# Weight unpacking, half of the score masks and the gate's carried columns leave VectorE, in a newly drawn order

## The chip, the cores and the metric

The kernel runs on one NeuronCore of a Trainium2 chip. Five engines work from queues of their own: TensorE (PE in the profile; PEld is its weight loads), VectorE (DVE), ScalarE (ACT), GpSimd (POOL) and SyncE (SP), which issues all the DMAs. An engine takes its instructions strictly in the order in which the program holds them. The metric is the device time of one execution in microseconds (us).

## The reference

Two layers, all in float32. The first is a recurrence over 768 time steps, for 4 batches and 8 heads of size 40; the second is a gated layer with a width-3 convolution.

```python
for t in range(S):                                   # attention part, B=4 H=8 S=768 D=40
    y[:, :, t] = einsum('bhd,bhde->bhe', rt, state)
    Sa = einsum('bhde,bhe->bhd', state, at)
    state = state * wt[:, :, None, :] - einsum('bhd,bhe->bhde', Sa, bt)
    state = state + einsum('bhd,bhe->bhde', vt, kt)

x = y.transpose(0, 2, 1, 3).reshape(B, S, H * D)     # [4, 768, 320]
h = maximum(x @ w_in, 0)                             # d_ff = 1024
conv = sum_k conv_w[k] * h_padded[:, k:k+S]          # 3 taps along time
out = (h / (1 + exp(-conv))) @ w_out
```

The weights `w_in`, `conv_w` and `w_out` come as float64 words, and the kernel turns them into float32 itself.

## The kernel before

The recurrence is cut into 24 chunks of 32 steps (`C = 32`). Inside a chunk it is written as matrices: scores between the chunk's vectors, a triangular system of 32 unknowns, and a state that is handed from chunk to chunk. Two neighbouring chunks form a pair (12 of them) and share loads, decays and one solve. The gated layer works on 12 windows of 64 steps, each in four quarters (`fp`) of the 1024 columns.

The work is cut into short parts, each a Python generator that stops at every `yield`:

- `we` (weights): a weight piece of 120 or 128 rows by 256 columns. The load, then `from_f64` (L211 to L236) on VectorE with eight instructions, the last two a product `ef` (L232) and a sum `tf` (L235); then ScalarE rounds it to the high part (L253) and GpSimd subtracts for the low part (L255). There are 23 pieces with the convolution's; two can be on their way at a time.
- `de`, `dd` (decays, decayed): running products of `w` by VectorE's scans (L369, L376) and the scaled `a`, `k`, `b`.
- `sc` (scores): products of `a` with `k` and `b` (tile `ps`), masked by VectorE into `at` (L437). `at[:, c, 0]` is for `k`, `at[:, c, 1]` for `b`.
- `si`, `so` (solve_in, solve): the `b` half of the scores goes through DRAM (`bd`) and comes back as `bb`, one system on each partition; the solve is then 31 steps of two elementwise instructions (L480, L486), followed by stores and loads through DRAM (`xd`, `tt`). `VSOL` says which solves run on VectorE; the others run on GpSimd.
- `ch` (chain): the step of the recurrence. TensorE's products `pp`, `pu` and `pn`, VectorE's sum of the state (L562), GpSimd's product with the decay (L568).
- `rt`, `vt`, `ut`, `st`, `pa`, `ou`, `fi` (rturn, vturn, uturn, sturn, pairs, outputs, finish): the chunk's output, scaled and split into a high and a low part (`xh`, `xl`; L665, L667) for the gated layer.
- `pk`, `mi`, `mo` (pack, moe_in, moe_out): per window a few copies by DMA, then per quarter eight float32r products for each of two column blocks (`ph`, L700), Relu on ScalarE into `hb` (L714), the three taps (L721 on ScalarE, L729 on VectorE), the sigmoid (L734), the gate's product (L736), its split (L740, L743), and the output matmuls (`po`, L754). `hb` holds two columns more than the window, carried from the window before: L712 copies them in from `hend`, L716 copies the new last two out.

What sets the order is a list of tokens written by hand or drawn by a planner, `ORDER`: `de1.0` advances part 0 of the decays of pair 1 to its next `yield`, `so0*2` advances solve 0 by two pieces. `emit_all` goes through the list and emits the instructions in just that order, and `put` only enforces what must precede what. So each engine's queue is the list as far as it concerns that engine.

```python
VSOL = range(0, 12, 2)
...
    def advance(key):
        a = acts[key]
        for other, n in a[3].get(a[2], ()):
            while acts[other][2] < n:
                advance(other)
```

Of the kernel before, what the change touches and what calls it, by code (L numbers as in the profile page):

```python
# [20 lines left out]
VSOL = range(0, 12, 2)  # L21
# [18 lines left out]
    st1*2 sc4 we6 so1 we8*4 we9 we10 ch1 lv3 rt1 we9 st1*2 ut1 pa1 lr2 ou1 ha4 ld3*2 we10 so1*3 fi0  # L40
    vt2 we10 fi0 fi1 de3.0 sc4 sc5 we9 we10 sc5 ch1 de3.1 we9 de3.1 ha4 we11 we12 lr3 rt2 fi1 st2*2
    fi1 we11 we12 we11*2 ro0 we13 we12*2 ha5 st2 we13 we14 ha5 ld4 so1 we13 dd3.0*3 dd3.1*3 we14*2
    ch2 si2 so2 ch2 pk0 ut2 so2*2 pa2 vt3 sc6 so2*2 st2 ou2 ch2 ro0 rt3 mi0.0*3 so2*2 mi0.0*2 ch2
    st3*2 we13 mi0.1*2 st3 ld4 so2 ld4 we14 lv4 we15 we16 ch3*2 sc6 sc7 ut3 we15 st3 we15 sc7 fi2*3
    lr4 mi0.0 pa3 mi0.0 ch3 we15 ch3 we16 mi0.0 we17 mi0.1 mi0.2 we17*2 mi0.2 so2 ch4 si3 we16 so3
    ou3 ha6 we16 we18 de4.0 we18 ha6 ha7 st4 fi3*2 we17 we19 de4.0 we18 mi0.1 we19 vt4 st4*3 lv5
    de4.1 ch4 ut4 so3 ch4 dd4.0 rt4 we18 we20 de4.1 we20 mi0.2 so3 we20 pa4 vt5 ch4 ch5 so3 mi0.2
    ch5 fi3 ha7 we19*2 we21*2 ut5 we20 we22*2 ou4 st5*2 mi0.1 st5 lr5 rt5 so3 we22 ld4 ld5 de5.0
    mi0.1 we21 ch5 we22 mi0.3 we21 mi0.0*2 so3 mi0.1*2 mi0.3 pa5 mi0.3 pk1 dd4.0*2 dd4.1 mi0.1*2
    dd4.1 st5 mi0.2 sc8 fi4*2 ld5 dd4.1 ou5 mi0.2 lv6 mi0.3 so3*2 sc8 mi0.2 sc9 mi0.2*2 ha8*2 ha9  # L50
    fi4 fi5 ld5 de5.0 de5.1 ha9 sc9 mi0.2 dd5.0 mi0.3 dd5.0 de5.1 lv7 mi1.0*3 mi1.1 ld5 dd5.0 dd5.1
    sc10 so3 si4 mi0.3 lr6 dd5.1*2 ch5 mi0.3 lr7 mi0.3 mi1.1*2 mi1.0*3 mi1.1 mi1.2 vt6 sc10 mi0.3
    mo0.0 sc11 mi0.3 mi1.1 mi1.0*2 mi1.1 ch6 st6 mi1.2 ch6*2 sc11 mi1.1*2 mo0.0*2 ch6 mo0.0 mo0.1*5
    ld6 ut6 rt6 ch7 mi1.1 so4 ld6 so4*2 pa6 vt7 st6 fi5*2 st6 so4*2 mi1.0 so4 mi1.2 st6 mi1.3 so4
    mi1.2 so4 lv8 ou6 mi1.0 mo1.0 mi1.2 mi1.3*2 st7*2 ch7 ut7 mi1.1 st7*2 rt7 ch7*2 mo1.0 pa7
    mi1.3*2 fi6*2 pk2 lr8 mi1.2*2 ou7 mi1.2 rt8 so4 si5 ch8 st8*2 mi1.2 mi1.3 mi1.2 mi1.3 ch8*2 lv9
# [946 lines left out]
```

## Time and profile before

| | |
|---|---|
| median of 3 runs | 708.97 us (708.5 to 709.71) |
| the profiled execution | 708.08 us, span 706.4 us |
| busy over the span: TensorE | 560.7 us, 79% |
| VectorE | 538.4 us, 76% |
| ScalarE | 350.7 us, 50% |
| GpSimd | 353.2 us, 50% |
| granted clock of TensorE | 0.906 of full speed |

The span is the time from the first to the last instruction. Rows that name a line give instruction, output and inputs, shapes, count, busy time, the mean in ns, then the idle time of the engine just before them and what ended it. Rows of a window give for each engine the busy time and the number of instructions in it. The profile's slices are 706.4 / 40 = 17.7 us long.

### The profile page before, as it was taken

How to read it: one execution, taken by the hardware profiler on the slowest of the kernel's cores; microseconds unless marked ns; L12 is line 12 of the kernel's file. 1: busy time of each engine (PE TensorE's matmuls, PEld its weight loads, DVE VectorE, ACT ScalarE, POOL GpSimd, SP SyncE). 2: the span in 40 equal slices, each digit the busy share in tenths (PEclk: the TensorE clock that was granted, in tenths of full speed). 3: DMA queues.
4: the chain of work that ended last, by engine and by line, in shares of the span. 5: the costliest groups of instructions: out<-in, count | busy, mean ns of one | idle time of the engine just before them, and what ended most of it. 6: DMA issues, size and time to landing. Idle time of an engine off the chain costs nothing. (4 is left out here: it accounts for less than half of the span.)

```text
span 706.4 us, 29930 instructions
## 1 busy us (share of the span) xinstructions
PE 560.7 (79%) x13021; PEld 497.9 (70%) x13021; DVE 538.4 (76%) x1261; ACT 350.7 (50%) x792; POOL 353.2 (50%) x582
## 2 busy tenths in 40 slices
PE   4444764677687898988977996899998977899886
...
DVE  6689889998999896657795578987979894456571
...
POOL 2001884037786235783234884236985028863321
PEclk9766777997799998989999998999998999999998
...
GB/s 139 120 117 108 103 112 102 95 94 144 22 41 107 56 72 79 94 81 82 82 20 89 86 86 106 81 60 69 89 62 91 6 54 94 29 51 32 21 30 19
DMA packets 242402, 53.40 MB, mean 76 GB/s; under 512 B 229000, under 2 KB 238112, under 8 KB 242272
## 3 DMA queue, kind: packets, MB, share of 16 engines
...
q8 instruction: 102, 1.67, 1.0%
...
## 5 line engine op out<-in xcount | busy, mean ns | idle before, releaser
L729 DVE SCALAR_TENSOR_TENSOR cc<-hb,cw,cc 128x256 f32<-128x256 f32 x192 | 106.3, 575 | 13.7 <-ACT cc L721 10.2
L568 POOL TENSOR_TENSOR s<-s,wc 120x360 f32<-120x360 f32 x88 | 75.8, 891 | 69.4 <-DVE s L562 69.4
L486 POOL TENSOR_TENSOR xx<-xx,st 128x126 f32<-128x126 f32 (+22 forms) x186 | 83.1, 447 | 14.6
L480 POOL TENSOR_TENSOR st<-xx,bb 128x126 f32<-128x126 f32 (+22 forms) x186 | 79.4, 427 | 21.1 <-DMA bb<-bd 8.4
L700 PE MATMUL ph<-xh,wih 120*128 120x256 f32 x288 | 56.6, 306 | 11.3 <-ACT hb L714 11.3
L486 DVE TENSOR_TENSOR xx<-xx,st 128x126 f32<-128x126 f32 (+22 forms) x186 | 54.2, 291 | 6.4
L480 DVE TENSOR_TENSOR st<-xx,bb 128x126 f32<-128x126 f32 (+22 forms) x186 | 53.6, 288 | 7.2 <-DMA bb<-bd 1.7
L736 DVE TENSOR_TENSOR cc<-cc,hb 128x512 f32<-128x512 f32 x48 | 40.8, 857 | 21.7 <-ACT cc L734 21.5
L562 DVE TENSOR_TENSOR s<-pn,s 120x360 f32<-120x360 f32 x88 | 40.6, 522 | 20.6 <-PE pn L549 20.6
L700 PEld LDWEIGHTS ph<-xh,wih 120*128 120x128 f32 x288 | 41.8, 194 | 15.0 <-ACT hb L714 13.1
L734 ACT ACTIVATE cc<-cc 128x512 f32<-128x512 f32 x48 | 30.4, 636 | 43.6 <-DVE cc L729 43.5
L667 POOL TENSOR_TENSOR xl<-xf,xh 120x384 fp32r<-120x384 f32 x24 | 26.8, 1117 | 45.2 <-ACT xh L665 41.5
L721 ACT ACTIVATE cc<-hb,cw 128x256 f32<-128x256 f32 x96 | 43.5, 506 | 8.7 <-DVE hb L712 2.9
L602 PE MATMUL pt<-ident,s 120*120 120x120 f32 x276 | 40.6, 279 | 6.4 <-DVE s L562 3.2
L427 ACT ACTIVATE ap<-ah,hmask 120x384 f32<-120x384 f32 (+1 forms) x72 | 36.6, 576 | 17.4 <-DVE ah L391 10.1
L604 ACT COPY sn<-pt 120x360 f32<-120x360 f32 x92 | 38.9, 471 | 12.2 <-PE pt L602 11.8
L714 ACT ACTIVATE hb<-ph 128x512 f32<-128x512 f32 x48 | 28.8, 600 | 27.2 <-PE ph L700 23.4
L579 ACT ACTIVATE rp<-pr,hmask 120x384 f32<-120x384 f32 x72 | 36.7, 586 | 6.9 <-PE pr L576 6.5
L700 PE MATMUL ph<-xl,wih 120*128 120x256 f32 x192 | 39.3, 287 | 0.0
L533 PE MATMUL pu<-psb,tt 32*32 32x40 f32 x1536 | 22.5, 209 | 19.6 <-ACT psb L527 16.1
L602 PEld LDWEIGHTS pt<-ident,s 120*120 120x120 f32 x276 | 31.2, 143 | 9.0 <-DVE s L562 3.5
L533 PEld LDWEIGHTS pu<-psb,tt 32*32 32x32 f32 x1536 | 18.7, 114 | 24.5 <-ACT psb L527 17.7
...
## 6 DMA issues: line engine op xcount, KB each, us to landing
...
```

The costliest lines, as they stand in the source:

```text
L480: eng.tensor_tensor(t3, xx[:, 0:nj, i : i + 1].to_broadcast([128, nj, nt]), bb[:, i : i + 1, i + 1 :].to_broadcast([128, nj, nt]), ALU.mult,)
L486: eng.tensor_tensor(xx[:, 0:nj, i + 1 :], xx[:, 0:nj, i + 1 :], t3, ALU.add)
L533: nc.tensor.matmul(pu[quad(bi), hc], tt[quad(bi), c, h, :], psb[quad(bi), hc], start=(h == 0), stop=True, skip_group_check=True,)
L562: nc.vector.tensor_tensor(new, pn[bi][:GR], old[bi], ALU.add)
L568: nc.gpsimd.tensor_tensor(n4, n4, w4, ALU.mult)
L579: nc.scalar.activation(out=rp[:, :, h, :], in_=pr[:GR], func=AF.Copy, scale=hmask[:, h : h + 1])
L602: nc.tensor.transpose(pt[:GR, g, :], old[bi][:, g, :], ident[:GR, :GR])
L604: nc.scalar.copy(sn, pt[:GR])
L700: nc.tensor.matmul(ph[:, j], l[:, fs], x, start=(j == 0 and i == 0), stop=(i == len(passes) - 1), skip_group_check=True,)
L721: nc.scalar.activation(out=cc[:, j], in_=hb[:, j, :, 1 : W + 1], func=AF.Copy, scale=cw[:, 1, f : f + 1],)
L729: nc.vector.scalar_tensor_tensor(out=cc[:, j], in0=hb[:, j, :, x : W + x], scalar=cw[:, x, f : f + 1], in1=cc[:, j], op0=ALU.mult, op1=ALU ...
L736: nc.vector.tensor_tensor(cc, cc, hb[:, :, :, 1 : W + 1], ALU.mult)
```

## The change

Three jobs change their engine, and the order is drawn anew.

- In each weight piece ScalarE multiplies the low word `m` by 2^-44, and GpSimd makes the product with `e` and the sum. VectorE keeps six of eight instructions.
- In the scores VectorE masks only the `k` half. ScalarE writes the `b` half with the sign turned and unmasked; the solve reads only the entries that the mask leaves. The signed mask `trin` is gone.
- The gate's copies of the two carried columns, into `hb` and out to `hend`, run on ScalarE.
- `VSOL` goes from the even solves to 0, 3, 5, 7, 9, 11, so solves 1 and 2 both run on GpSimd, and from 3 on the odd ones on VectorE.

```diff
-VSOL = range(0, 12, 2)
+VSOL = (0, 3, 5, 7, 9, 11)
...
 ORDER = """
-    ld0 de0.0*2 ld0*2 de0.1 ld0 ld1 de0.1 we0 dd0.0*3 dd0.1*2 sc0 dd0.1 we0 ld1*2 lr0 sc0 sc1 lr1
+    we0*2 ld0*2 de0.0*2 de0.1*2 ld0 dd0.0*2 ld0 we1 dd0.0 dd0.1*3 we0 sc0 ha0*2 ld1 de1.0 we1 de1.0
...
-    trin = cp.tile([128, 2, 1, C], F32, name="trin")
-    nc.vector.tensor_copy(trin[:, 0, 0], tri)
-    nc.vector.tensor_scalar(
-        out=trin[:, 1, 0], in0=tri, scalar1=-1.0, scalar2=None, op0=ALU.mult
-    )
...
         tf, ef = t.bitcast(F32), e.bitcast(F32)
+        nc.scalar.activation(out=m.bitcast(F32), in_=m, func=AF.Copy, scale=2.0**-44)
         V.scalar_tensor_tensor(out=tf, in0=e, scalar=896.5, in1=tf, op0=ALU.is_ge, op1=ALU.mult)
         V.tensor_scalar(out=e, in0=t, scalar1=-(1 << 23), scalar2=None, op0=ALU.bitwise_and)
-        V.scalar_tensor_tensor(
-            out=ef, in0=m, scalar=2.0**-44, in1=ef, op0=ALU.mult, op1=ALU.mult
-        )
-        V.tensor_tensor(tf, tf, ef, ALU.add)
+        nc.gpsimd.tensor_tensor(ef, m.bitcast(F32), ef, ALU.mult)
+        nc.gpsimd.tensor_tensor(tf, tf, ef, ALU.add)
...
+        nc.scalar.activation(out=at[:, c, 1], in_=ps[:, 1], func=AF.Copy, scale=-1.0)
         nc.vector.tensor_tensor(
-            at[:, c], ps, trin.to_broadcast([128, 2, H, C]), ALU.mult,
+            at[:, c, 0], ps[:, 0], tri.unsqueeze(1).to_broadcast([128, H, C]), ALU.mult,
         )
...
-                    nc.vector.tensor_copy(hb[:, :, :, 0:2], he)
+                    nc.scalar.copy(hb[:, :, :, 0:2], he)
...
-        nc.vector.tensor_copy(he, hb[:, :, :, W : W + 2])
+        nc.scalar.copy(he, hb[:, :, :, W : W + 2])
```

What this does to the queues, at three places. The rows give line, operation, output and inputs, and the output's shape; line numbers of the new kernel are some four lower.

VectorE, the second weight piece (`wi10`), before and now:

```order
L217 TENSOR_SCALAR wi10q<-wi10r 120x256
L221 TENSOR_SCALAR wi10q<-wi10r 120x256
L225 SCALAR_TENSOR_TENSOR wi10q<-wi10r,wi10q 120x256
L228 TENSOR_SCALAR wi10s<-wi10r 120x256
L230 SCALAR_TENSOR_TENSOR wi10q<-wi10q 120x256
L231 TENSOR_SCALAR wi10q<-wi10q 120x256
L232 SCALAR_TENSOR_TENSOR wi10q<-wi10s,wi10q 120x256
L235 TENSOR_TENSOR wi10q<-wi10q 120x256
```

```order
L213 TENSOR_SCALAR wi10q<-wi10r 120x256
L217 TENSOR_SCALAR wi10q<-wi10r 120x256
L221 SCALAR_TENSOR_TENSOR wi10q<-wi10r,wi10q 120x256
L224 TENSOR_SCALAR wi10s<-wi10r 120x256
L227 SCALAR_TENSOR_TENSOR wi10q<-wi10q 120x256
L228 TENSOR_SCALAR wi10q<-wi10q 120x256
```

The last two rows are no longer VectorE's; they stand in GpSimd's queue.

GpSimd, around the start of its second solve (`xx3` before, `xx2` now; `s20` to `s33` are the state's four batches after chain steps 2 and 3, `wl` parts end in `il` and `ol`), before and now:

```order
L255 TENSOR_TENSOR wol_114<-wo2q_2118,woh_113 128x256
L568 TENSOR_TENSOR s30_2360<-s30_2360,wc2_677 120x360
L568 TENSOR_TENSOR s31_2362<-s31_2362,wc2_677 120x360
L568 TENSOR_TENSOR s32_2364<-s32_2364,wc2_677 120x360
L568 TENSOR_TENSOR s33_2366<-s33_2366,wc2_677 120x360
L710 MEMSET hb02_2413 128x8x2
L473 CAST xx3_2479<-xini_98 128x512
L480 TENSOR_TENSOR st3_0_2481<-xx3_2479,bb3_2475 128x31
```

```order
L229 TENSOR_TENSOR cvq_1596<-cvs_1597,cvq_1596 24x128
L230 TENSOR_TENSOR cvq_1596<-cvq_1596 24x128
L250 TENSOR_TENSOR wil_109<-wi23q_1575,wih_108 120x256
L229 TENSOR_TENSOR wo0q_1619<-wo0s_1620,wo0q_1619 128x256
L230 TENSOR_TENSOR wo0q_1619<-wo0q_1619 128x256
L564 TENSOR_TENSOR s20_1749<-s20_1749,wc1_227 120x360
L564 TENSOR_TENSOR s21_1751<-s21_1751,wc1_227 120x360
L564 TENSOR_TENSOR s22_1753<-s22_1753,wc1_227 120x360
L564 TENSOR_TENSOR s23_1755<-s23_1755,wc1_227 120x360
L469 CAST xx2_1938<-xini_95 128x512
L476 TENSOR_TENSOR st2_0_1940<-xx2_1938,bb2_1819 128x31
```

GpSimd's second solve is solve 2, a step of the chain earlier than solve 3, and products and sums of weight pieces stand ahead of the state's multiplications.

The carried columns of a window's quarter: VectorE before, where a copy to `hend` stands between the instructions of solve 4, and ScalarE now:

```order
L480 TENSOR_TENSOR st_27_4166<-xx_4007,bb_3613 128x56
L486 TENSOR_TENSOR xx_4007<-xx_4007,st_27_4166 128x14x4
L716 COPY hend<-hb_3785 128x16
L480 TENSOR_TENSOR st_28_4170<-xx_4007,bb_3613 128x45
L486 TENSOR_TENSOR xx_4007<-xx_4007,st_28_4170 128x15x3
```

```order
L708 COPY hb_3766<-hend 128x8x2
L575 ACTIVATE rp_3772<-pr_3768,hmask 120x3x128 x3
L580 COPY rt_3776<-pr_3768 120x384
L710 ACTIVATE hb_3766<-ph_3422 128x8x64
L712 COPY hend<-hb_3766 128x16
```

Both copies now stand in the queue of the engine that runs the Relu (L710), one ahead of it and one behind.

More of the change, by code (lines that the diff above doesn't have):

```diff
@@ L40 @@
[L40 to L56, printed above, removed]
@@ L102 @@
[L102 to L105 removed]
+    we0*2 ld0*2 de0.0*2 de0.1*2 ld0 dd0.0*2 ld0 we1 dd0.0 dd0.1*3 we0 sc0 ha0*2 ld1 de1.0 we1 de1.0
+    sc0 sc1 ld1 de1.1 sc1 lr0 we1 de1.1 we0 we2*4 ha1*2 we1 we3*2 we4*2 si0 so0 dd1.0 so0 ld1 we3
@@ new lines @@
+    we20*2 we19 ld5*2 vt4 st4 we19 we21*2 we20*2 we22 so2 ch4 we22 ch4 we22 we21 si3 so3*3 ch4 so3
+    st4*2 we21 ut4 pa4 so3*2 st4 lv6 ou4 vt5 ch4 st5*2 we22 mi0.1 st5 ch5 mi0.0*2 ch5 so3 sc9 mi0.2
+    lr5 rt5 so3 fi3 lr6 pk1 mi0.2*2 ch5 mi0.1 mi0.3 mo0.0*2 ut5 mi0.3 mi1.0 mi0.2 mi1.0 ld5 sc9
+    mi1.0 mi1.1 mi0.2 ch5 mi0.3 st5 mi0.3*2 pa5 mi0.2 so3 ch6 si4 ld5 fi4 mi0.3*2 ch6*2 lv7 fi4 ou5
+    mi1.0 ha8*2 de5.0 fi4 fi5 de5.0 fi5 vt6 mi1.0 de5.1 ld6 mi1.1 rt6 mi1.1*2 de5.1 ch6 mi1.0 ut6
+    mo0.0*2 mo0.1 st6 mi1.1*3 fi5 mi1.0 ha9 mi1.2 so4*3 lv8 st6 mi1.0 mi1.2 ch7 mi1.2 de6.0 mo0.1
@@ new lines @@
+    st6*2 mi1.3 mi1.2 mo0.1*2 mi1.0*2 dd5.0 ch7*2 mi1.1 mi1.3 mi1.2 pa6 mi1.1 ut7 ha9 ou6 vt7
+    dd5.0*2 dd5.1*2 lr7 mi1.2 dd5.1 rt7 mo1.0 mi1.3*2 sc10 so4*2 mi1.1 fi6 st7 mi1.3 mi1.2 so4*2
+    mi1.2 pa7 st7*2 sc10 vt8 so4 st7 mi1.3 sc11 ou7 mi1.2*2 pk2 ha10 mi2.0 mi1.3*2 mi2.0*2 fi6
+    mi2.1*2 mo1.0 ld6 fi6 fi7 ch7 de6.0 ld6*2 dd6.0 ha10 mi1.3 ha11 sc11 mi2.0*2 lr8 ha11 mi2.0
+    dd6.0*2 mo0.1 de6.1 lv9 mi1.3 rt8 mi2.1*2 st8*3 de6.1 dd6.1 mi2.0*2 lr9 dd6.1 st8 so4 ch8 si5
+    mi2.1 ch8 mi2.1 ut8 mo0.0 dd6.1 sc12 ch8 pa8 mi2.1 sc12 vt9 mi2.1 ou8 ch8 rt9 mo1.0*2 mo1.1
@@ new lines @@
+    de10.0 mi5.3*3 fi14*2 fi15 mi6.1*2 ha18 ha19 mo5.0 de10.0 de10.1 dd10.0*2 de10.1 rt16 ld10 ha19
+    dd10.0 so8 si9 dd10.1*2 ld11 mi5.2 mi6.0*3 mo5.0*2 dd10.1 mi6.1 vt16 lr17 ld11 fi15 mi6.1*2
+    mi6.2 ch15 ch16 mi6.0 ch16 mi6.0 sc20 mo5.1 ch16 ut16 mi6.1*2 sc20 pa16 mi6.2*2 sc21 lr18 ch16
+    st16 so9 lv17 mi6.3*2 mo5.1 mi6.3*2 so9*2 st16 so9 mo5.1*2 mi6.1 so9*3 st16*2 so9 vt17 ch17
+    de11.0 mi6.0*2 fi15 mo6.0 mo5.1 mi6.2*2 ou16 st17*2 ch17 ut17 pk7 mi7.0 rt17 ch17 mi6.1 ch17
+    mi6.2 lv18 sc21 mi6.3 mo5.0 so9 pa17 st17*2 fi16 mi6.2*3 si10 lv19 mi7.0*2 fi16 mi6.3 mi7.1 ld11
```

105 lines of the change are left out of this document (52 added, 53 removed).

## The prediction

> **What bounds the kernel now.** I read the page first (spans, the 40 slices), then busy time by stage, then the lists of waits by stage, and last the timeline of TensorE for the places where a step of the recurrence begins.
>
> ```profile
> span 706.4 us, 29930 instructions
> ...
> PE 560.7 (79%) x13021; PEld 497.9 (70%) x13021; DVE 538.4 (76%) x1261; ACT 350.7 (50%) x792; POOL 353.2 (50%) x582
> ...
> PE   4444764677687898988977996899998977899886
> ...
> DVE  6689889998999896657795578987979894456571
> ...
> POOL 2001884037786235783234884236985028863321
> PEclk9766777997799998989999998999998999999998
> ...
> GB/s 139 120 117 108 103 112 102 95 94 144 22 41 107 56 72 79 94 81 82 82 20 89 86 86 106 81 60 69 89 62 91 6 54 94 29 51 32 21 30 19
> ```
>
> No engine is full over the span, but the slices (17.7 us each) show two stages. In the first eleven or so VectorE stands at 8 and 9 tenths and TensorE at 4 to 7; later TensorE stands at 8 and 9 and VectorE falls. Cut at 200 us, the busy times are these (columns: TensorE, its weight loads, VectorE, ScalarE, GpSimd, granted clock, DMA share, GB/s):
>
> ```profile
> 0.00:200.00 200.00, 120.79 (x2866) 103.19 (x2867) 172.44 (x442) 72.35 (x168) 85.12 (x164) 0.79 0.54 102
> 200.00:706.00 506.00, 439.89 (x10157) 394.71 (x10155) 365.97 (x820) 278.38 (x625) 268.08 (x418) 0.95 0.36 65
> ```
>
> VectorE is 86% busy in the first stage and TensorE 87% in the second. What they wait for in their own stage is small. The longest wait of VectorE in the first 200 us, the longest of TensorE after 200 us, and the longest of GpSimd in the first 220 us are:
>
> ```profile
> DVE suf L369 <- ACT wx L365: 3.6, 2, 3.4
> ```
>
> ```profile
> PE ph L700 <- ACT hb L714: 11.3, 9, 4.5
> ```
>
> ```profile
> POOL wil L255 <- ACT wih L253: 58.3, 5, 26.0
> ```
>
> So VectorE's queue is the bound of the first stage, TensorE's work (with some 66 us of scattered waits) that of the second, and GpSimd spends the first stage mostly waiting for weight pieces to reach it. The chain of waits, last, goes back only to 686.6 us; it begins and ends so, with the last gate and output matmuls between, and says nothing on the rest:
>
> ```profile
> 686.56 0.02 issue
> ...
> 702.88 0.41 ACT oe L803
> ```
>
> **The change part by part.** I price each part, then ask which stage it lies in. The busy times of four lines in the first 200 us, in this order: L232 and L235 (the two VectorE instructions that leave each weight piece), L255 (GpSimd's subtraction on a tile of the same size) and L253 (ScalarE's rounding copy of that size).
>
> ```profile
> 0.00:200.00 200.00, 10.90 (x23) 0.79 0.54 102
> ```
>
> ```profile
> 0.00:200.00 200.00, 10.31 (x23) 0.79 0.54 102
> ```
>
> ```profile
> 0.00:200.00 200.00, 16.18 (x20) 0.79 0.54 102
> ```
>
> ```profile
> 0.00:200.00 200.00, 8.27 (x21) 0.79 0.54 102
> ```
>
> Weight pieces: VectorE loses 10.9 + 10.3 = 21 us, all in the first stage. GpSimd gains 46 instructions at 16.18 / 20 = 0.81 us, 37 us. ScalarE gains 23 at 8.27 / 21 = 0.39 us, 9 us, and is idle for 64% of that stage, so I cost it at nothing; if that cover were gone it would be the 9 us. The piece now crosses engines twice more: ScalarE waits for VectorE with the copies of the decays and the scaled keys queued behind it, and GpSimd waits for both with the state's multiplications (L568) and the solves behind it, for which TensorE waits in turn. That is GpSimd's line of the sum, below.
>
> ```profile
> L437 DVE TENSOR_TENSOR at<-ps,trin 128x512 f32<-128x512 f32 x24 | 16.4, 682 | 10.3 <-PE ps L411 10.2
> L562 DVE TENSOR_TENSOR s<-pn,s 120x360 f32<-120x360 f32 x88 | 40.6, 522 | 20.6 <-PE pn L549 20.6
> L729 DVE SCALAR_TENSOR_TENSOR cc<-hb,cw,cc 128x256 f32<-128x256 f32 x192 | 106.3, 575 | 13.7 <-ACT cc L721 10.2
> L712 DVE COPY hb<-hend 128x16 f32<-128x16 f32 x44 | 12.6, 289 | 0.3
> L716 DVE COPY hend<-hb 128x16 f32<-128x16 f32 x48 | 12.4, 264 | 16.6 <-ACT hb L714 16.5
> L270 ACT COPY cw<-pc 128x24 f32<-128x24 f32 x1 | 0.2, 178 | 0.3 <-PE pc L269 0.3
> ```
>
> Masking: of 512 columns VectorE keeps 256. No row has that size; from L437 and L562 the slope is (682 - 522) / (512 - 360) = 1.05 ns a column, so 682 - 256 x 1.05 = 0.41 us remain and 0.27 us go, 6.5 us over 24 steps, a third of it in the first stage. ScalarE takes 24 x about 0.39 = 9 us. The half that both engines now write is waited for by the store to DRAM ahead of each solve; ScalarE's part stands beside VectorE's, and I cost it at nothing. The two instructions that made the signed mask go as well; they stood at the start, where VectorE waits 3.4 us for its first data, and count as nothing.
>
> Carried columns: 92 copies, 12.6 + 12.4 = 25 us of VectorE, nearly all in the second stage, and with them 16.5 us in which VectorE stood at L716 waiting for ScalarE's Relu. On ScalarE they are ordered behind that Relu anyway. They cost it 92 x 0.18 (L270, the nearest small copy) = 16 us. In the second stage ScalarE is busy 278 of 506 us, so I put this at nothing; the other end, every copy delaying the Relu that TensorE waits for, would be the 16 us.
>
> The same for GpSimd's side of the pieces is not free, because the two engines get in each other's way. Shortest, median and longest of three VectorE groups:
>
> ```profile
> L729 DVE SCALAR_TENSOR_TENSOR cc<-hb,cw,cc x192: 469/485/1493, 153.7 to 688.6; 128x256 f32<-128x256 f32 x192
> ```
>
> ```profile
> L712 DVE COPY hb<-hend x44: 158/170/1078, 220.8 to 683.8; 128x16 f32<-128x16 f32 x44
> ```
>
> ```profile
> L614 DVE TENSOR_TENSOR ms<-pm,tri x24: 676/682/694, 73.7 to 662.3; 128x512 f32<-128x512 f32 x24
> ```
>
> A copy of 16 columns takes 170 ns or 1078, while L614, which reads TensorE's banks, never varies. The long ones lie across a GpSimd instruction. L729 has a mean of 575 against a median of 485 (its group's row above), so 90 ns in 485, 19%, is the price of a GpSimd that is busy half the time. In the first stage GpSimd would go from 85 of 200 us (43%) to (85 + 37) of some 185 (66%): 23 points, 23 / 50 x 19% = 9% more on VectorE's remaining 150 us. The bounds are 0 and 13 us; as L562- and L614-like work is spared I take two thirds, 9.
>
> The Trainium skill, "GPSIMD Engine Reference", section "Specifications", says that GpSimd's access to the on-chip memory is shared with VectorE, and that they contend when a VectorE instruction has two inputs there or runs in a two-port mode. The rows above agree (1078 against 170 ns; 694 against 676 where one input is in TensorE's banks). Were the sharing complete, 46 instructions that took 0.46 us on the one and take 0.81 on the other would make the common queue 46 x 0.35 = 16 us longer instead of VectorE's shorter, and the sum would stay near 708 instead of falling to 694; that is the third case below, worked out there from rows alone.
>
> Order: the tokens are drawn anew, so like must be compared with like. I take the first matmuls of the recurrence's steps 4 and 6 (TensorE's timeline):
>
> ```profile
> 158.68 0.39 PE L514 MATMUL pp<-s,ah 120*32 120x120 f32 x2 [1.70 <-POOL s L568]
> ```
>
> ```profile
> 227.79 0.62 PE L514 MATMUL pp<-s,ah 120*32 120x120 f32 x16
> ```
>
> I counted what stands ahead of them in each engine's queue, each instruction at its group's median or mean here. Ahead of step 4 the new order has 14 us more on TensorE, 14 less on VectorE, 52 more on GpSimd (solve 2 and 35 of the 46 new instructions). Ahead of step 6: TensorE 12 less, VectorE 33 less (21 of the pieces, 2 or 3 of the masks, the rest two decays and gate work that now stand behind), GpSimd 32 more (all 46; two solves either way). By VectorE, step 6 comes at 227.8 - (33 - 9) / 0.86 = 200 us. TensorE then has 12 us of work more to do, 12 / 0.87 = 14 us at the second stage's rate, so the kernel is 28 - 14 = 14 us ahead. The solves show whether GpSimd can follow: solves 0, 1, 2, 3, then 11 (length of the stretch, busy time on VectorE, on GpSimd):
>
> ```profile
> 30.70:53.30 22.60, 16.18 (x63) 0.00 (x0) 0.62 0.67 120
> 64.80:105.80 41.00, 0.00 (x0) 27.81 (x63) 0.75 0.59 113
> 126.90:149.50 22.60, 18.28 (x63) 0.00 (x0) 0.92 0.44 96
> 163.90:215.90 52.00, 0.00 (x0) 28.75 (x63) 0.84 0.34 70
> ...
> 591.20:624.30 33.10, 0.00 (x0) 25.84 (x63) 0.95 0.19 39
> ```
>
> and what else GpSimd's queue holds there:
>
> ```profile
> L568 POOL TENSOR_TENSOR s<-s,wc 120x360 f32<-120x360 f32 x88 | 75.8, 891 | 69.4 <-DVE s L562 69.4
> ...
> L667 POOL TENSOR_TENSOR xl<-xf,xh 120x384 fp32r<-120x384 f32 x24 | 26.8, 1117 | 45.2 <-ACT xh L665 41.5 <-PE pn L549 3.7
> ```
>
> A solve takes 23 us on VectorE and 33 to 52 on GpSimd. Solves 1 and 2 now both lie on GpSimd. Solve 1 starts at about 68 (3 us later, for the work that VectorE has more ahead of it). Between the two stand 8 x 0.89 (L568) + 2 x 1.12 (L667) + 10 x 0.81 (pieces) = 17 us. Each solve at the 41 us of solve 1, solve 2 ends at 68 + 41 + 17 + 41 = 167; GpSimd's 35 us up to step 6, with a fifth for contention 42, end at 209. But solve 1 took 41 us beside a VectorE that was dense with pieces; by the order VectorE now has 10 us of work queued over its length instead of 25, so 36 us a solve, between 33 and 41, is nearer, and step 6 is free at 199. The two engines then agree on 200. Solve 3 runs on VectorE meanwhile. Solve 11 goes from 33 to 23 us; it is hidden behind gate matmuls in both, so nothing. SyncE's queue now starts with a weight piece of 240 KB ahead of the decays' input, 1.7 us at the first slice's 139 GB/s, while VectorE's first piece fills that wait: 0 to 1.7, in the range.
>
> Second stage: TensorE's work is the same and VectorE is not what it waits for, so I leave its 87%. Sum: 708.1 us (the profiled execution; span 706.4 and 1.7 around it; the median of the runs is 708.97) - 14 = 694 us.
>
> **The rivals.** Second: the freed VectorE also shortens the second stage. Of the 25 + 16.5 us of copies and their wait there, enough arrives to lift TensorE from 87% to 89%: 439.9 / 0.89 = 494 instead of 506, 12 us more, 682 us. For it: the waits of TensorE are for ScalarE, which waits for VectorE in turn. Against it: ScalarE itself gets 25 us more there.
>
> Third, the common queue: GpSimd takes VectorE's place in the first stage, and the gain is nil. With solves 1 and 2 at 41 and 46 us step 6 falls at 68 + 41 + 17 + 46 + 42 = 214, where the 14 us are used up: 706 to 710 us. For it: VectorE and GpSimd together have 33 - 32 = 1 us less ahead of step 6, so as much work for the pair. Against: in the first 200 us GpSimd is busy 85 us only, and 58.3 us of its waits are for pieces that now come to it earlier.
>
> Fourth, slower, by one mechanism: GpSimd runs its queue in order, and beside a dense VectorE each solve on it takes 52 us, as solve 3 did. Then solve 2 ends at 68 + 52 + 17 + 52 = 189 and step 6 comes at 231, 3 us late and with 14 us of TensorE's time less done: 17 us lost, 725 us. It decides when step 6 comes after 214. Against it: solve 3's 52 us held other GpSimd work too, as the whole of that stretch shows (GpSimd is the fifth engine column):
>
> ```profile
> 163.90:215.90 52.00, 40.65 (x1099) 35.75 (x1092) 47.01 (x97) 28.56 (x70) 41.43 (x80) 0.84 0.34 70
> ```
>
> **How the numbers follow.** 694 us has 45%, its own range 688 to 701; 682 us 20%; 706 to 710 us 18%; 725 us 17%. About 0.2% (1.4 us) can be told from no change, which is 707.5 to 710.4. The first two are faster; the third I split 7, 7 and 4. Faster 72%, same 7%, slower 21%. The range from 677 to 712 leaves out the fourth case and little below the second.
>
> **What would show it.** Right: VectorE near 490 us busy, GpSimd near 390, ScalarE near 385; solve 2 on GpSimd ended by 167; step 6 at 199 to 209; the last stage at 87%. Wrong: GpSimd at 9 tenths from 70 to 200 us with VectorE below 8; weight pieces waiting for GpSimd's last subtraction; TensorE's waits for ScalarE's Relu well over 11 us.

## The result, and the profile after

The changed kernel takes 732.88 us (median of 4 runs, 730.25 to 737.58) against 709.34 us for the kernel before, run beside it. The ratio is 1.0339, interval 1.0281 to 1.0397: 3.4% slower, where 694 us were forecast. The profiled execution below was the longest of the four (737.58 us), so its span differs from before's by 29.5 us and not by the 23.5 of the medians.

The page of the changed kernel, its span, busy times and slices (18.4 us each):

```profile
span 735.9 us, 29914 instructions
...
PE 559.3 (76%) x13021; PEld 497.8 (68%) x13021; DVE 514.2 (70%) x1121; ACT 377.9 (51%) x931; POOL 387.9 (53%) x628
...
PE   5135775874277998897979889998878887897786
...
DVE  7987537579796557977487985589755738876552
...
POOL 2506876788535677227881228871329755323321
```

VectorE stood at 8 and 9 tenths from the third to the eleventh slice before. Now it falls to 5, 3 and 5 in between (fifth, sixth and eighth slice), and TensorE has a hole (4, 2, 7) in the tenth to twelfth, about 165 to 220 us. The windows up to the first matmul of step 6 tell what became of the ramp; before, then changed, with that matmul (TensorE's timeline) behind:

```profile
0.00:227.80 227.80, 143.23 (x3332) 122.92 (x3332) 197.78 (x488) 89.21 (x206) 105.27 (x197) 0.81 0.53 100
```

```profile
0.00:229.70 229.70, 129.95 (x3073) 110.97 (x3077) 173.36 (x410) 93.27 (x225) 134.65 (x242) 0.77 0.51 97
```

```profile
229.74 0.73 PE L510 MATMUL pp<-s,ah 120*32 120x120 f32 x24
```

VectorE (third busy time) was busy 197.8 of 227.8 us and is now busy 173.4 of 229.7. It has 24.4 us less to do, and step 6 is no earlier: VectorE stands idle 56.3 us instead of 30.0. TensorE has done 13.3 us less. The idle time lies in the middle; 50 to 150 us before and changed, and VectorE's longest waits there in the changed kernel:

```profile
50.00:150.00 100.00, 62.44 (x1703) 53.57 (x1701) 89.75 (x237) 37.65 (x90) 46.65 (x87) 0.77 0.50 101
```

```profile
50.00:150.00 100.00, 68.05 (x1803) 59.08 (x1807) 62.72 (x142) 43.95 (x106) 69.12 (x138) 0.76 0.51 100
```

```profile
DVE at L433 <- ACT at L432: 8.2, 3, 6.6
DVE ms L610 <- PE pm L406: 6.5, 2, 6.2
DVE xf L653 <- PE pq L651: 6.0, 1, 6.0
DVE s L554 <- PE pn L545: 3.4, 1, 3.4
```

VectorE goes from 10 us of idle time in this stretch to 37. It waits at the head of its queue for products of steps 2 and 3 and for ScalarE's half of the masks. Before, it began five weight pieces between 70 and 110 us; in the new order none stands there, as ten were done by 70 us and the next begins at 111. The last seven (`wo3` to `wp1`) then come in one block. GpSimd's timeline ahead of solve 2 (first row) and from its end on, and ScalarE's around its eviction `psb` for step 4 (start, length, what ended the idle time before):

```profile
123.83 0.72 POOL L230 TENSOR_TENSOR wo0q<-wo0q 128x256 f32<-128x256 f32 x1
...
166.54 0.73 POOL L250 TENSOR_TENSOR wol<-wo1q,woh 128x256 fp32r<-128x256 f32 x1
167.23 0.72 POOL L250 TENSOR_TENSOR wol<-wo0q,woh 128x256 fp32r<-128x256 f32 x1
167.91 0.77 POOL L229 TENSOR_TENSOR wo2q<-wo2s,wo2q 128x256 f32<-128x256 f32 x1
...
172.15 0.73 POOL L229 TENSOR_TENSOR wo3q<-wo3s,wo3q 128x256 f32<-128x256 f32 x1 [0.75 <-DVE wo3q L228]
...
177.98 0.77 POOL L229 TENSOR_TENSOR wo4q<-wo4s,wo4q 128x256 f32<-128x256 f32 x1
```

```profile
189.18 0.42 ACT L226 ACTIVATE wp0s<-wp0s 128x256 f32<-128x256 int32 x1 [1.73 <-DVE wp0s L224]
189.51 0.39 ACT L248 CAST woh<-wo7q 128x256 fp32r<-128x256 f32 x1
189.80 0.43 ACT L523 ACTIVATE psb<-pp 128x320 f32<-128x320 f32 x1
```

The first row shows the sum of piece `wo0`, done at 124.6 us; its subtraction stood behind solve 2 in GpSimd's queue and ran at 167.2. From there the pieces follow each other some 3 us apart until 195 us, on all three engines, with the chain's own small instructions between them or behind. That is TensorE's hole (its timeline, four waits):

```profile
172.52 0.86 PE L406 MATMUL ps<-ap,kt 120*32 120x96 f32 x16 [3.74 <-DVE kt L394]
177.16 1.08 PE L406 MATMUL ps<-ap,bt 120*32 120x96 f32 x22 [3.55 <-DVE bt L394]
190.28 1.29 PE L529 MATMUL pu<-psb,tt 32*32 32x40 f32 x64 [7.80 <-ACT psb L523]
204.77 0.89 PE L587 MATMUL put<-ident,u 128*120 128x128 f32 x3 [9.49 <-DVE s L558]
```

24.6 us in four waits: two for VectorE's scaled keys between pieces, one for a ScalarE copy behind the pieces' copies, one for VectorE's sum of the state behind the last pieces and the first half of solve 3.

After step 6 there is a second loss. From there to the end TensorE needed 417.5 us of work in 478.6 us before (87.2%); it now has 429.4 in 506.2 (84.8%). The largest part of the lower share lies between 500 and 600 us of the changed kernel: 81.4%, where before has 87.5% in the same 100 us and 91.3% ten us earlier:

```profile
490.00:590.00 100.00, 91.28 (x2245) 81.98 (x2244) 85.01 (x186) 55.00 (x124) 58.40 (x87) 0.97 0.34 63
```

```profile
500.00:600.00 100.00, 81.40 (x1804) 73.69 (x1797) 68.76 (x148) 53.90 (x134) 52.88 (x86) 0.93 0.32 56
```

The 29.5 us of span by these rows: step 6 is 1.9 us late, the 11.9 us of work that TensorE has more to do behind it cost 13.7, and the lower share costs the other 14.

### The profile page after: what moved, and what is told of

It is laid out like the page before. It is cut to its first block, busy times and chain, and to the rows that moved or that the text cites. A ratio compares the mean times of both kernels' runs of the same rounds, so it can differ in the third digit from the quotient of the medians.

```text
span 735.9 us, 29914 instructions
## 1 busy us (share of the span) xinstructions
PE 559.3 (76%) x13021; PEld 497.8 (68%) x13021; DVE 514.2 (70%) x1121; ACT 377.9 (51%) x931; POOL 387.9 (53%) x628
## 3 DMA queue, kind: packets, MB, share of 16 engines
q1 hardware_dynamic: 242272, 51.50, 38.1%
## 4 chain that ended last, share of the span: by engine, by line
PE 40%; DVE 33%; ACT 14%; issue 6%; DMA 4%; SPq 2%; POOL 1%; DVEq 0%; ACTq 0%; POOLq 0%
PE po L750 7%; DVE cc L725 7%; PE ph L696 7%; DVE st L476 5%; DVE xx L482 5%; PE pn L545 4%; PE py L634 4%; ACT rp L575 2%; DVE s L558 2%; PE py L625 2%; PE ps L406 2%; PE pu L529 2%; DVE cc L732 2%; PE pm L406 2%; PE pt L598 2%
## 5 line engine op out<-in xcount | busy, mean ns | idle before, releaser
L725 DVE SCALAR_TENSOR_TENSOR cc<-hb,cw,cc 128x256 f32<-128x256 f32 x192 | 114.3, 617 | 29.6 <-ACT cc L717 26.2
L476 DVE TENSOR_TENSOR st<-xx,bb 128x126 f32<-128x126 f32 (+22 forms) x186 | 57.9, 311 | 9.6 <-DMA bb<-bd 3.7
L732 DVE TENSOR_TENSOR cc<-cc,hb 128x512 f32<-128x512 f32 x48 | 38.6, 809 | 29.7 <-ACT cc L730 29.4
L640 ACT COPY ysb<-py 128x320 f32<-128x320 f32 x24 | 10.2, 426 | 59.3 <-PE py L634 59.3
L710 ACT ACTIVATE hb<-ph 128x512 f32<-128x512 f32 x48 | 28.9, 604 | 16.4 <-PE ph L696 16.4
```

The costliest lines, as they stand in the source:

```text
L476: eng.tensor_tensor(t3, xx[:, 0:nj, i : i + 1].to_broadcast([128, nj, nt]), bb[:, i : i + 1, i + 1 :].to_broadcast([128, nj, nt]), ALU.mult,)
L725: nc.vector.scalar_tensor_tensor(out=cc[:, j], in0=hb[:, j, :, x : W + x], scalar=cw[:, x, f : f + 1], in1=cc[:, j], op0=ALU.mult, op1=ALU ...
L732: nc.vector.tensor_tensor(cc, cc, hb[:, :, :, 1 : W + 1], ALU.mult)
```

## The experiments

Beside every one of them `before` was measured again; its median was 709 to 712 us, so differences of two microseconds between kernels measured at different times say nothing.

**One part at a time.** First the moves without the order, and the order without the moves.

```diff
 # e1: the changed kernel, with before's order and split
-VSOL = (0, 3, 5, 7, 9, 11)
+VSOL = range(0, 12, 2)
 ORDER = """
-    we0*2 ld0*2 de0.0*2 ...
+    ld0 de0.0*2 ld0*2 de0.1 ...
```

> All three moves between engines, with the order and the solves' engines of before. If the loss lies in GpSimd's queue (weight pieces stuck behind a solve and then bunched), it shows here too, since the pieces still pass GpSimd twice more: 720 to 740 us. If the loss is the new order's own, this is 695 to 712 us.

735.47 us, ratio 1.0357 (1.0327 to 1.0387). The moves alone, in the old order, lose as much as the change.

```diff
 # e2: the kernel before, with the new order and split
-VSOL = range(0, 12, 2)
+VSOL = (0, 3, 5, 7, 9, 11)
 ORDER = """
-    ld0 de0.0*2 ld0*2 de0.1 ...
+    we0*2 ld0*2 de0.0*2 ...
```

> The new order and the new choice of solves, with the engines of before. If GpSimd's queue is the cause, pieces no longer pass GpSimd in the middle and 705 to 720 us come out. If the order is the cause, it stays at 725 to 745 us, since VectorE has all its work back as well.

756.11 us, ratio 1.063 (1.0587 to 1.0673). The order and split alone lose 46 us, more than either expectation. So neither half is a gain by itself.

```diff
 # e3: the kernel before, with the weight pieces moved
+        nc.scalar.activation(out=m.bitcast(F32), in_=m, func=AF.Copy, scale=2.0**-44)
...
-        V.scalar_tensor_tensor(
-            out=ef, in0=m, scalar=2.0**-44, in1=ef, op0=ALU.mult, op1=ALU.mult
-        )
-        V.tensor_tensor(tf, tf, ef, ALU.add)
+        nc.gpsimd.tensor_tensor(ef, m.bitcast(F32), ef, ALU.mult)
+        nc.gpsimd.tensor_tensor(tf, tf, ef, ALU.add)
```

> Of the change only the weight pieces' move, in the old order. Theory of GpSimd's queue: 5 to 20 us slower than before (714 to 730). Theory of the order: the move by itself is harmless or a gain, 695 to 710 us.

735.69 us, ratio 1.0361 (1.0327 to 1.0396): all of e1's loss, and more than the 5 to 20 us that were expected of GpSimd's queue. As the order is before's, the steps can be laid side by side. Step 1 comes at the same time, step 2 is 11 us late, step 5 25.5, and from step 6 on the delay stays between 22 and 29 us to the end. The two jumps are the two GpSimd solves that have pieces in their queue. Solves 1 and 3 (length, VectorE's and GpSimd's busy time in the solve's own instructions) and GpSimd's longest waits for pieces within each, with the one of before's solve 3 last:

```profile
67.80:120.50 52.70, 0.00 (x0) 27.12 (x63) 0.73 0.42 84
180.00:243.00 63.00, 0.00 (x0) 25.96 (x63) 0.76 0.24 48
```

```profile
POOL wi13q L233 <- ACT wi13s L230: 5.3, 1, 5.3
```

```profile
POOL wo7q L233 <- DVE wo7q L232: 7.0, 1, 7.0
POOL wo6q L233 <- DVE wo6q L232: 3.3, 1, 3.3
```

```profile
POOL wol L255 <- ACT woh L253: 4.9, 3, 3.3
```

The solves' own instructions took 26 to 29 us in either kernel; the stretches went from 41 to 52.7 and from 52 to 63 us. Waiting for a weight piece in the middle of a solve is new in solve 1 (8.6 us in all, none before). In solve 3 it is not new: there it grows from 4.9 us to 12.4.

```diff
 # e4: the kernel before, with half of the mask on ScalarE
+        nc.scalar.activation(out=at[:, c, 1], in_=ps[:, 1], func=AF.Copy, scale=-1.0)
         nc.vector.tensor_tensor(
-            at[:, c], ps, trin.to_broadcast([128, 2, H, C]), ALU.mult,
+            at[:, c, 0], ps[:, 0], tri.unsqueeze(1).to_broadcast([128, H, C]), ALU.mult,
         )
```

> Of the change only the split mask, in the old order. In the changed kernel VectorE's mask instruction waits for ScalarE's, 26.0 us of idle VectorE in 14 waits. If those waits cost time: 712 to 725 us, with the same wait in the list. If they only stand where VectorE would have been idle anyway: 705 to 711 us.

706.92 us, ratio 0.9949 (0.9921 to 0.9977). VectorE waits 19.4 us in all for ScalarE's half here too, and the kernel is 3 us faster all the same, so on balance these waits cost it nothing.

```diff
 # e5: e4, and the carried columns on ScalarE
-nc.vector.tensor_copy(hb[:, :, :, 0:2], he)
+nc.scalar.copy(hb[:, :, :, 0:2], he)
...
-nc.vector.tensor_copy(he, hb[:, :, :, W : W + 2])
+nc.scalar.copy(he, hb[:, :, :, W : W + 2])
```

> Before's order and solver split, with two of the three moves: half of the mask on ScalarE and the gate's carried columns on ScalarE; the weight pieces stay as before. The half mask alone gave a ratio of 0.995. Theory A (the whole loss is the weight pieces' two instructions in GpSimd's queue): nothing here touches GpSimd's queue, so no slower than before, 700 to 707 us; the copies take 25 us of busy time and 16 us of waiting off VectorE, but VectorE is not what ends last after the ramp, so a gain of a few us at most. Rival B (ScalarE's load, 30 us more, delays the Relu and the eviction copies that TensorE waits for): 712 us or more. Rival C (VectorE's freed time lifts TensorE in the second stage, as one case of the forecast had it): 690 us or less.

706.69 us, ratio 0.994 (0.9912 to 0.9968). These two moves gain some 4 us, nearly all of it the mask's. This is the version that beats both kernels.

**What in a moved piece costs.**

```diff
 # e6: the kernel before; q2[:, 256:512] is read by nothing else, dmi is constant
+            c4 = dmi.unsqueeze(1).to_broadcast([128, 4, 64])[: d.shape[0]]
+            d4 = d.bitcast(F32).rearrange("p (a c) -> p a c", a=4)
+            nc.gpsimd.tensor_tensor(d4, c4, c4, ALU.mult)
+            nc.gpsimd.tensor_tensor(d4, d4, d4, ALU.add)
```

> The kernel before, unchanged in what it computes, with two GpSimd instructions of 128x256 added at each weight piece where the change puts its product and its sum: they read a constant and a part of the piece's buffer that nothing else uses, so that they wait for no other engine and no other engine waits for them; VectorE keeps all its work. Theory A1 (own time: each such instruction takes 0.75 to 0.9 us of GpSimd's in-order queue, ten of them stand in solve 1 and ten in solve 3): solve 1 grows from 40.9 to 49 us, solve 3 from 51.9 to 60, the end comes 16 to 20 us later, 725 to 730 us. Theory A2 (it is the product's wait for ScalarE and VectorE, 6.7 us in solve 1 and 11.3 us in solve 3 with the pieces moved): without that wait the two solves grow by less than 5 us each and the time is 715 us or less. Rival B (GpSimd and VectorE exclude each other on SBUF, so the added instructions slow VectorE in the whole ramp): over 735 us, with the delay spread over the steps instead of two jumps.

717.94 us, ratio 1.0109 (1.0076 to 1.0142), between A1 and A2: 7 us of the 26, with solve 1 at 47.4 and solve 3 at 55.3 us. VectorE keeps all its own work here, so the 7 us hold GpSimd's own time and what it slows on VectorE. That is the smaller part.

```diff
 # e7: e3 with this split; e8: the kernel before with it
-VSOL = range(0, 12, 2)
+VSOL = (0, 1, 2, 3, 4, 6, 8, 10)
```

> Before's order with the weight pieces moved and nothing else of the change, but solves 1 and 3 on VectorE instead of GpSimd (2 as before on VectorE, 5, 7, 9 and 11 on GpSimd): no solve stands beside a weight piece in GpSimd's queue. To be read against the same split without the pieces moved (the next kernel). Theory A (the pieces cost because they lie in the queue of a GpSimd solve): the difference of the two is within 5 us, or the moved pieces are faster. Rival B (the hop over three engines itself delays the weights, whatever GpSimd does besides): the moved pieces are slower by 15 us or more here too.

> The kernel before with solves 1 and 3 on VectorE instead of GpSimd and nothing else changed: the comparison for the kernel ahead of it. On VectorE a solve took 22 us alone, and VectorE is 8 to 9 tenths busy up to 180 us, so two more solves, 45 us, on it: theory A and rival B both expect slower than before, 720 to 745 us, as the ramp is VectorE's then.

735.40 us (ratio 1.0339, 1.0298 to 1.038) and 729.59 us (1.0264, 1.0228 to 1.0301): with no GpSimd solve beside them the moved pieces cost 5.8 us instead of 26, just above the 5 that theory A allowed and far from rival B's 15.

```diff
 # e9: e3 with product and sum in the piece's next step
         yield
+        nc.gpsimd.tensor_tensor(g, m[:rows].bitcast(F32), g, ALU.mult)
+        nc.gpsimd.tensor_tensor(tf, tf, g, ALU.add)
         nc.scalar.copy(dsth, f)
```

> Before's order and solver split with the weight pieces moved, as in the run of the pieces alone (735.7 us), but GpSimd's product and sum are issued one step of the piece later, together with ScalarE's copy, instead of right behind VectorE's and ScalarE's half. GpSimd does the same work; what differs is that other instructions stand ahead of the product while ScalarE and VectorE make its inputs. Theory A2 (two thirds of the loss, 18 of 26 us, is the product at the head of GpSimd's queue waiting for its inputs, 7 us in solve 1 and 11 us in solve 3, with the solve behind it; the added idle work without a wait cost 7 us): 715 to 724 us, with under 3 us of idle time before the product in each of the two solves. Theory A1 (GpSimd's own time is the loss): 735 us again. Rival B (the later product makes the piece later, and the weights come late to chain and projections): over 738 us.

732.63 us, ratio 1.031 (1.026 to 1.036): a miss for theory A2 in this form. The time is nearer A1's 735 us, though e6 had put GpSimd's own time at 7 us. Solve 1 was shorter than in e3 (42.8 against 52.7 us), but two pairs then stood between it and the state's product, so step 2 came only 2.3 us earlier than in e3. In solve 3 GpSimd waited 6.6 us for `wo7` again. Moving a wait along the same queue did not remove it.

```diff
 # e18: e5, with only twelve of the 23 pieces moved
+    STAY = ('wi02', 'wi12', 'wi22', 'wi03', 'wi13', 'wo4', 'wo5', 'wo6', 'wo7', 'wp0', 'wp1')
...
+        if moved:
+            # from_f64's lines as in the change, then return tf
```

> Before's order and split with the half mask and the copies on ScalarE (706.7 us), and the weight pieces moved as in the change, but only the twelve whose GpSimd part stood outside GpSimd's solves 1 and 3 in the trace of the moved pieces (wi00 to wi21, wi23, the convolution's piece, wo0 to wo3); the other eleven stay on VectorE. Theory A (a moved piece costs where it stands in the queue of a GpSimd solve that VectorE waits for, and nothing elsewhere): 700 to 709 us. Rival B (each moved piece costs about 1.1 us, 26 us over 23, wherever it stands): 717 to 723 us. Rival C (moved pieces outside the solves free VectorE, 0.9 us each): under 700 us.

709.81 us, ratio 0.9993 (0.9962 to 1.0024). Twelve pieces outside the solves cost 3 to 4 us against e5, a little more than theory A allowed. By subtraction the eleven others carry the rest of the 29 us between e5 and e1; they were not moved alone. Nothing was gained by the twelve either, so rival C falls too.

**The other direction.**

```diff
 # e11: e5, with the pieces' subtraction on VectorE
-nc.gpsimd.tensor_tensor(dstl, f, dsth.bitcast(F32), ALU.subtract)
+nc.vector.tensor_tensor(dstl, f, dsth.bitcast(F32), ALU.subtract)
```

> Before's order and solver split with the half mask and the copies on ScalarE (706.7 us), the weight pieces' product and sum on VectorE as before, and their last step, the subtraction that GpSimd did (0.73 to 0.93 us each, four within solve 1 and seven within solve 3), on VectorE as well: the opposite of the change. Theory A (GpSimd's queue at solves 1 and 3 sets the ramp): solve 1 loses 3.2 us of its queue, solve 3 5.4 us and up to 4.9 us of waiting, 694 to 702 us. Rival B (VectorE, 9 tenths busy in the ramp, is as tight, and takes 23 more instructions of 0.43 us at its worst place): 706 to 716 us.

709.73 us, ratio 0.9997 (0.9956 to 1.0038): rival B. Against e5, 23 subtractions less on GpSimd gain nothing and cost some 3 us. It fits a ramp in which both engines are tight and work taken off one is paid on the other; which wait pays was not traced.

**The new order.**

```diff
 # e10: the changed kernel, pieces as before
-        nc.scalar.activation(out=m.bitcast(F32), in_=m, func=AF.Copy, scale=2.0**-44)
...
-        nc.gpsimd.tensor_tensor(ef, m.bitcast(F32), ef, ALU.mult)
-        nc.gpsimd.tensor_tensor(tf, tf, ef, ALU.add)
+        V.scalar_tensor_tensor(
+            out=ef, in0=m, scalar=2.0**-44, in1=ef, op0=ALU.mult, op1=ALU.mult
+        )
+        V.tensor_tensor(tf, tf, ef, ALU.add)
```

> The changed kernel with the weight pieces put back on VectorE: its new order and solver split, its half mask and copies on ScalarE. The new order with all old engines took 756 us, with all new ones 733. Theory A (GpSimd's queue): the new order puts its solves 1 and 2 on GpSimd at 72 to 167 us with ten pieces' instructions in it, so without these it gains, 705 to 720 us. Rival B (the new order needs VectorE empty: it was drawn for it, and puts three chunks' products beside the pieces): with the pieces on VectorE it stays at 745 to 756 us, and the 23 us between 756 and 733 came from the pieces.

733.84 us, ratio 1.0324 (1.0276 to 1.0371): neither. In the new order the move of the pieces changes nothing (732.88 with it). Their GpSimd instructions stand outside its solves there, but for one pair at 148 us. The loss is that of the order with its split: against e5, which has the same engines, it is 27 us. VectorE's hole is there without any moved piece, and so are TensorE's four waits (21.2 us instead of 24.6) and the lower share after step 6 (50 to 150 us, then up to step 6 and from there to the end):

```profile
50.00:150.00 100.00, 68.76 (x1836) 59.05 (x1834) 68.07 (x170) 42.40 (x98) 57.12 (x122) 0.79 0.56 105
```

```profile
0.00:228.30 228.30, 133.65 (x3077) 113.49 (x3081) 178.30 (x456) 86.03 (x202) 100.39 (x196) 0.77 0.53 98
228.30:731.80 503.50, 426.06 (x9958) 384.49 (x9948) 340.37 (x712) 284.36 (x706) 252.28 (x386) 0.95 0.34 62
```

From e2 to e10 mask and copies alone gain 22 us. So, with the order taken first, the account of the change is: order and split +46, mask and copies -22, pieces -1, together +23. With the moves taken first it is: mask and copies -4 (e5), pieces +29 (e1), order and split -3. The parts are not independent, and neither account is the only one.

```diff
 # e12: e10 with before's split; e13: e5 with the new split
-VSOL = (0, 3, 5, 7, 9, 11)
+VSOL = range(0, 12, 2)
 # and the reverse
```

> The changed kernel's new order with the half mask and the copies on ScalarE and the pieces on VectorE (733.8 us with the new split of solves), but before's split: solves 0, 2, 4, 6, 8, 10 on VectorE and the odd ones on GpSimd. With old order and old split these engines took 706.7 us. Theory O (the place of the work in the order costs the 27 us: VectorE idle 32 us between 50 and 150 us, and the pieces wo3 to wp1 in one block of 25 us ahead of solve 3): the split changes little, 725 to 745 us. Rival S (the split costs it: solve 2 takes 33 us on GpSimd where VectorE took 22, and the last solve is VectorE's): 706 to 715 us.

> Before's order with the half mask and the copies on ScalarE and the pieces on VectorE (706.7 us), but the changed kernel's split: solves 0, 3, 5, 7, 9, 11 on VectorE, 1, 2, 4, 6, 8, 10 on GpSimd. Theory O (the order): 705 to 720 us; solve 2 ends some 11 us later on GpSimd, solve 3 earlier on VectorE. Rival S (the split): 725 us or more.

862.37 us (1.2081, 1.2 to 1.2163) and 814.88 us (1.1439, 1.1395 to 1.1483). In e12 neither theory has the time. In e13 rival S has its 725 us or more, but the same rival wanted 706 to 715 in e12. Each order is good here only with its own split, and the 27 us cannot be divided between the two. In e13 the steps are 24 us behind before's at step 6 and 107 at the last one: in that order this split goes on costing time long after the last weight piece.

```diff
 # e14: the changed kernel, e15: e10; the steps of we10 to we22 spread ahead
-    ... ha5 we10 de3.1 ch1 st2 we10 we11*2 ld3 ld4 we10*2 we12 fi1*2 we11 ...
+    we10 lv2 rt1 st1 we10 so1*2 we11 so1 ch1 we11 ut1 so1 we10 pa1 vt2 ...
```

> The changed kernel (732.9 us) with one edit of its order: the steps of the weight pieces from the eleventh on keep their sequence, but stand evenly spread between the end of the tenth piece and step 2's end (about 75 to 150 us) instead of mostly behind it. Everything else, the pieces' two GpSimd instructions too, as in the change. Theory O (the block of pieces at 168 to 197 us, one behind the other, holds solve 3 and the state products of steps 4 and 5): step 4 comes 8 to 15 us earlier than 181 us, and the time is 715 to 725 us. Rival Q (GpSimd's queue: the pieces' product and sum then stand within solves 1 and 2 on GpSimd, and lengthen them by 10 us each, as with the old order): solve 2 ends 10 us later, and the time is 733 us or more.

> As the run ahead of it, with the pieces on VectorE (733.8 us without the spread): VectorE has 32 us of idle time between 50 and 150 us in that kernel, in which the nine pieces moved ahead, 3.2 us each, find room. Theory O: step 4 earlier by 10 to 20 us, 712 to 722 us. Rival: the VectorE waits there are for products of steps 2 and 3 that follow each other, and pieces put ahead of them only delay these: 733 us or more, step 4 no earlier.

773.68 us (1.0859, 1.0822 to 1.0896) and 749.51 us (1.0523, 1.0479 to 1.0567). Theory O falls in this form. On VectorE the pieces now stand ahead of what solve 2 needs, which starts at 144.3 instead of 129.8 us. With the pieces moved it costs 24 us more: solve 2 starts only at 161.4 us, behind the pairs of `wo3`, `wo4` and `wo5` and their waits.

```profile
POOL wo3q L230 <- ACT ut L590: 12.2, 1, 12.2
...
POOL wo5q L230 <- ACT woh L249: 3.7, 1, 3.7
...
POOL wo4q L230 <- ACT wo4s L227: 2.1, 1, 2.1
```

The longest of them is not the dearest. GpSimd's next work, the state's product, needed VectorE's sum, which ended at 144.5 us, and began at 147.8: some 9 of the 12.2 us would have been waited anyway. From 151.9 to 161.4 us GpSimd has only the pairs of `wo4` and `wo5` and their waits.

```diff
 # e16: the changed kernel, e17: e10; we16 to we22 behind, and mo0.0 with them
-    ... we16 ha7*2 mi0.1 ... we22 we21 si3 so3*3 ch4 so3 ...
+    ... ha7*2 mi0.1 ... si3 so3*3 ch4 so3 st4*2 ut4 pa4 so3*2 we16 st4 ...
```

> The changed kernel (732.9 us) with the last seven weight pieces (wo3 to wp1) moved the other way: behind most of solve 3 and the state products of steps 4 and 5, spread up to the first projection back, whose first two steps move behind them. Theory P (VectorE's seven pieces at 168 to 197 us stand ahead of solve 3 and of the state products, and that order is the ramp's loss): solve 3 starts some 20 us earlier than 193 us, step 6 comes at 205 to 215 us instead of 229.7, and the time is 712 to 724 us. Rival W (TensorE then has no projection back to do until the weights are there, and the last pieces' GpSimd instructions stand beside solve 4): step 6 comes earlier, but the time stays at 730 us or more.

> The same order with the pieces on VectorE (733.8 us with the changed kernel's order). Theory P: 712 to 724 us. Against the run ahead of it: if GpSimd's queue at solve 4 is what the pieces meet there, this one is 5 us or more faster than that.

743.82 us (1.0494, 1.0423 to 1.0564) and 738.23 us (1.0407, 1.0327 to 1.0486). Half of theory P came: in e17 step 4 comes at 170.8 instead of 181.3 us, step 5 at 195 instead of 213.4. But step 6 stays at 230.5 us (228.3 in e10). ScalarE's seven `woh` copies now stand in a row at the head of its queue, six of them waiting for VectorE, and the eviction for step 5 behind them; ScalarE's and then TensorE's timeline:

```profile
199.83 0.41 ACT L250 CAST woh<-wo3q 128x256 fp32r<-128x256 f32 x1 [4.43 <-DVE wo3q L232]
203.00 0.41 ACT L250 CAST woh<-wo4q 128x256 fp32r<-128x256 f32 x1 [2.77 <-DVE wo4q L232]
...
219.86 0.44 ACT L525 ACTIVATE psb<-pp 128x320 f32<-128x320 f32 x1
```

```profile
220.35 1.29 PE L531 MATMUL pu<-psb,tt 32*32 32x40 f32 x64 [23.67 <-ACT psb L525]
```

In each of the three places tried, the pieces held up a queue in which work of the chain stood behind them. None of them gained time. That the block costs the 27 us is therefore read from the traces and not shown by a run that got them back.

The price of moving the pieces, over all pairs of kernels that differ in nothing else:

| | on VectorE | moved | price, us |
|---|---|---|---|
| old order, ten pairs beside GpSimd's solves 1 and 3 | 709.9 | 735.7 (e3) | 26 |
| old order, mask and copies too | 706.7 (e5) | 735.5 (e1) | 29 |
| the same, only twelve pieces outside the solves | 706.7 (e5) | 709.8 (e18) | 3 |
| old order, solves 1 and 3 on VectorE | 729.6 (e8) | 735.4 (e7) | 6 |
| new order | 733.8 (e10) | 732.9 | -1, within the noise |
| new order, pieces spread ahead of solve 2 | 749.5 (e15) | 773.7 (e14) | 24 |
| new order, last pieces behind solve 3 | 738.2 (e17) | 743.8 (e16) | 6 |

Each is a net price: the same move takes work off VectorE. It is 24 us and more in the rows where pairs stand in a GpSimd solve or hold up its start, and 6 at most elsewhere. The new order's row is the exception to watch: there too pairs stand directly ahead of solves 1 and 2, but solve 2 ends only 3 us later for it (166.6 against 163.3) and the block of pieces behind it decides.

## Why the prediction was wrong

The step that failed is "By VectorE, step 6 comes at 227.8 - (33 - 9) / 0.86 = 200 us". The 24 us in it were right as a sum: VectorE has 197.8 - 173.4 = 24.4 us less to do. That is partly luck. e10, with the pieces on VectorE, already has 19.5 us less (178.3), where 12 of the 33 were counted for mask and order, and the pieces then take off 4.9 us, where 21 less 9 for contention were forecast. The 0.86 was wrong. It was the share of an order in which VectorE always had a weight piece to work on, and I carried it to an order that I had counted but not read for what stands at the head of the queue. The share fell to 173.4 / 229.7 = 0.755. At 0.868, before's own share, 173.4 us of work would have taken 199.7.

"Second stage ... I leave its 87%" failed as well: 84.8%, 14 us. e10 has the lower share without the moved pieces (426 of 503.5 us, 84.6%). e1, e3, e5, e6, e9, e11 and e18, in the old order with the old split, keep their delay against before from step 6 on to within some 6 us; with the new split it grows in e13. So it is the order's or the split's. Which of its queues costs it, at 500 to 600 us, was not isolated and stays open.

Term by term:

- GpSimd's line held in part. Solve 2 ended at 166.6 us, where the sign said 167 and the working, at 36 us a solve, gives 157. The solves took 31.5 and 38.1 us, but the first began at 72.1 us instead of 68, and 24.9 us lay between the two instead of 17. Further, "step 6 is free at 199" by GpSimd took solve 3 to run on VectorE "meanwhile". VectorE came to it only at 193.4 us, behind the pieces.
- The fourth case had the right side and 725 us, but not by its mechanism, which wanted solve 2 to end at 189 us. Step 6 did fall where it put it, 229.7 against 231.
- "TensorE then has 12 us of work more to do, ... 14 us": 11.9 and 13.7 us.
- The pieces: 21 us off VectorE for 37 on GpSimd, priced by each engine's load. e6 puts the load at 7 us in the old order; e3, e7 and e18 show that most of the price there is where an instruction that waits for another engine stands in GpSimd's queue. I had named the solves behind such a wait, and priced none of it.
- Contention: 9 us forecast, 0 to 13. In e3 VectorE is busy 524.7 us, where 538.4 - 21.2 = 517.2 would be left: 7.5 us. Between e10 and the changed kernel it is 21.2 - 4.5 = 16.7 over the whole span, above the 13 us that were the upper bound. So in the new order most of what the pieces took off VectorE came back. Why it is more there was not isolated.
- Mask: 0.41 us forecast, 0.424 measured (L433). Costing ScalarE's half at nothing was right in the old order (e4). In the new order VectorE waits 26.0 us in all for it, 8.2 of them between 50 and 150 us; what these waits cost was not isolated, and e4 has 19.4 us of them at no cost. Carried columns: nothing forecast, nothing measured in the old order.

Of the signs of being right, GpSimd's load came (387.9 us, near 390) and VectorE's did not: 514.2 us where some 490 were forecast, so the rest of its work took longer. Of the signs of being wrong, "VectorE below 8" came, with GpSimd nowhere at 9 tenths, and so did the wait for a subtraction on GpSimd (`wo0`), though e10 shows that the block of pieces comes without any moved piece. TensorE's waits for the Relu rose only from 11.3 to 13.6 us after step 6. A sign for the case that came, VectorE idle with its pieces still ahead of it, I had not thought of.
